# Routed expert kernel: the low halves of w1 prepared earlier, a softmax set eight steps later, one weight request moved ahead of another

## The chip, the cores and the metric

The kernel runs on one core of a Trainium2 chip. The metric is the device time of one execution in microseconds (us). Every run here is of the whole kernel, from its inputs in DRAM to its output in DRAM.

## The reference

The reference has two stages. The first is a causal convolution along the sequence whose seven weights differ at every position and head; they come from a softmax over the seven raw weights. The second is a mixture of 16 experts in 4 groups of 4: each token picks a group, then an expert of it, runs through that expert's two matrices and is scaled by the product of the two gate weights.

```python
w = np.exp(weight_gen - np.max(weight_gen, axis=-1, keepdims=True))
w = w / (np.sum(w, axis=-1, keepdims=True) + 1e-09)          # B=8, S=2880, 8 heads, K=7
out = np.einsum('bshk,bskhg->bshg', w, x_unf)                # x_unf: the 7 last rows of x, D=192
x = out.reshape(23040, 192)
g_idx = np.argmax(x @ w_group, axis=1)
...
e_idx = np.argmax(xg @ w_expert[g], axis=1)
...
h = np.maximum(xg[mask_e] @ w1[g, e], 0.0)                   # w1: 192 x 1024
ye = h @ w2[g, e]                                            # w2: 1024 x 192
out[tok_idx] = combined[:, None] * ye
```

## The kernel before

**Convolution.** The 23040 tokens lie as 128 partitions of 180. They are worked in 15 groups of 12 columns (two chunks of 6). For each group the SP queue loads the raw weights `wt` and the rows `xin` (`load_group`, lines 119 and 129; two buffers of each, so the load of group g+1 waits until group g-1 is done with its buffers). `softmax` (lines 260 to 280) turns `wt` into weights: maximum (L265), subtraction (L267), exponential on ScalarE (L268), sum (L273), reciprocal (L277), product (L279). `conv` multiplies by each of the seven taps on VectorE (L294). In the first three groups TensorE adds the products up (L335) and ScalarE copies the sums out (L338); from group 3 on VectorE adds them itself (L312).

**Routing.** `logits` transposes the convolved rows and scores them on TensorE (L392, L393, L375, L419), with copies on ScalarE between (L385, L399, L411, L422). `ranks` picks group and expert on VectorE (L346 to L360, then `oh` at L449), counts on TensorE (L459, L460) and gives each token a row in DRAM; GpSimd scatters the rows (L503). `table` (L528 to L586) then lists blocks of rows for a round.

**Experts.** 14 rounds give a list of blocks in a fixed order. Round 0 (after group 1) has ten singles (128 rows, block numbers 0 to 9), the rounds after it have doubles (256 rows, from block 10 on), the last one has ten triples, six doubles and two singles and a remainder. A block loads its rows `xb` (L779), its first matrix and its second (L803), and runs gemm1 (L907) and gemm2 (L945) in four or eight units. A single loads the first matrix straight into a tile `wa` (L790; three tiles in turn). A larger block loads it raw (`raw`, L792 and L799) and splits it into a rounded part, made by ScalarE (L816, L825), and a rest, made by VectorE (L840). One of the loads at L799 reads `w1lo` from DRAM.

**Low halves.** `w1lo` holds the rest of the last 64 rows of w1 and is made once by `halves`, in eight pairs of experts. For pair k: SP fetches it (`fetch`, L610); ScalarE makes the negative rounded copy (L602); SP stores the fetched rows to DRAM (L604); GpSimd adds the negative copy onto them with an accumulating DMA (L605). The tiles for this are borrowed from `wa`, `wc` and `raw`. `HALVES` holds the due time of each fetch on the planner's own clock; the low half of pair k-1 is made right after fetch k.

**Order.** The program order on TensorE, ScalarE, VectorE and SP is written out by a planner while the kernel is built. It keeps a clock for each engine with a fixed cost for each step. `front` yields the steps of the convolution; between two of them `beside` moves low halves, then the next group's softmax (the list `side`), then the routing. `blocks` writes out the expert units and fills with steps of `front` up to TensorE's clock plus a lead. Requests for loads stand in a list, and `pump` writes them out in order on the SP queue, which runs in program order, so a load that waits holds all that stand behind it. `state["slots"]` becomes true when the first double is taken up. `FIRST` is 2.

Of the kernel before, what the change touches and what calls it, by code (L numbers as in the profile page):

```python
# [22 lines left out]
AHEAD = (1.0, 1.0, 2.5)  # L23
HURRY = 12
SPACED = range(2, 15)
HALVES = (36.0, 42.0, 48.0, 54.0, 60.0, 66.0, 72.0, 78.0)
WHOLE = 12
SINGLE = tuple((k,) for k in range(7))
MIXED = ((0, 1), (2,), (3,), (4,), (5,), (6,))
# [12 lines left out]
def conv_moe_kernel(ctx: ExitStack, tc: tile.TileContext, x, wgen, w_group, w_expert, w1, w2, out):  # L42
# [27 lines left out]
    ENDS = [r[0] for r in ROUNDS]  # L70
# [6 lines left out]
    FIRST = ENDS[0]  # L77
# [151 lines left out]
    state = {"slots": False, "open": False, "unit": 0, "starve": False, "ph": 0, "hold": False}  # L229
# [360 lines left out]
    def halves():  # L590
# [9 lines left out]
        def lower_half(k):  # L600
            e, hi, raw = 2 * k, his[k % len(his)], raws[k]
            nc.scalar.activation(out=hi, in_=raw, func=AF.Copy, scale=-1.0)  # L602
            low = w1lo[e:e + 2].rearrange("e p f -> (e p) f")
            nc.sync.dma_start(out=low, in_=raw)  # L604
            nc.gpsimd.dma_start(out=low, in_=hi.bitcast(F32), accum_op=ALU.add)  # L605
            run("pool", 1.1, run("act", 1.0))

        def fetch(k):
            for h in range(2):
                nc.sync.dma_start(out=raws[k][h * HP:(h + 1) * HP, :], in_=w1v[2 * k + h, P:D, :])  # L610

        yield NEXT
        for k, raw in enumerate(raws):
            yield Until(HALVES[k])
            fetch(k)
            if k == 0:
                continue
            lower_half(k - 1)
        yield Until(HALVES[-1] + 6.0)
        lower_half(len(raws) - 1)  # L620
# [16 lines left out]
    def front():  # L637
        side = []
        set_up()
        load_group(1)  # L640
        next(slow[0][0])
        yield from softmax(0, 0, SC)
        rest = softmax(0, SC)

        def pace(g):
            return 99 if g <= FIRST else HURRY if g < MAIN + 3 else 8 if g in ENDS else 2

        def beside(g, n):
            rush = g >= FIRST and not grp[FIRST - 1].routed
            if not rush:  # L650
                for q in list(slow):
                    yield from move(slow, q, 2)
            for q in side[:1]:
                if not rush:
                    yield from move(side, q, 3)
            yield from routing(g)

        def routing(g):
            if ranking:
                yield from move(ranking, ranking[0], pace(g))  # L660
            if scoring and (not ranking or g < FIRST):
                yield from move(scoring, scoring[0], pace(g) if scoring[0][2].chunks == 2 or g >= FIRST - 1 else 3)

        def settle(g):
            while not grp[g].routed:
                qs = ranking or scoring
                q = qs[0]
                yield from move(qs, q, 99)
                if qs and qs[0] is q and q[1] is not None:
                    yield Until(q[1][1]) if q[1][0] == "time" else NEXT  # L670

        for g in range(ENDS[-1]):
            o = grp[g]
            o.routed = False
            scoring.append([logits(g, o), None, o])
            for n, c in enumerate(conv(g, o)):
                yield c
                if g == 0 and n < 6:
                    for c in islice(rest, None if n == 5 else 1):
                        yield c  # L680
                if n == (2 if state["slots"] else 0) and 1 <= g < ENDS[-1] - 1:
                    load_group(g + 1)
                if n >= (12 if state["slots"] else 4) and not o.ahead and g + 1 < ENDS[-1] and g != FIRST - 1:
                    o.ahead = True
                    side.append([softmax(g + 1), None])
                yield from beside(g, n)
                if g == FIRST - 1 and n in (7, 8):
                    if n == 7:
                        soft = softmax(FIRST)
                    yield next(soft)  # L690
            if g == FIRST - 1:
                for n, c in enumerate(soft):
                    yield c
                    yield from beside(g, n)
            yield from finish_all(side)
            if g:
                yield from settle(g - 1)
        yield from settle(ENDS[-1] - 1)
# [59 lines left out]
    def plain(n):  # L758
        return order[n][1] == 1
# [229 lines left out]
    def blocks(n0, n1, paced):  # L989
# [24 lines left out]
        def ask_w(n):  # L1014
            ask(n, 1)
            ask(n, 2)
# [66 lines left out]
        for i in range(len(units) + LAG):  # L1083
            if i < len(units):
                n, u = units[i]
                last = units_of(n) - 1
                gemm1(cur, u)
                queue.append((cur, u))
                nxt_at = i + last + 1 - u
                if nxt_at < len(units):  # L1090
                    if u == 0:
                        pump(units[nxt_at][0])
                        nxt = block(nxt_at)
                        prep_d(nxt)
                    if u == 1:
                        prep_x(nxt, 0)
                    if u == last // 2 + 1 and nxt.nt > 2:
                        prep_x(nxt, 2)
                if u == last and i + 1 < len(units):
                    cur = nxt  # L1100
            asks = []
            if i >= LAG:
                b, u = queue.pop(0)
                gemm2(b, u)
                if u == units_of(units[i - LAG][0]) - 1:
                    finish(b)
                    if i - LAG + 1 < len(units):
                        asks.append(units[i - LAG][0] + 3)
            if i < len(units):
                n, at = units[i]  # L1110
                end = at == last
                if end and n + 3 < n1 and (plain(n + 3) or plain(n + 2)):
                    ask_w(n + 3)
                    if not plain(n + 3):
                        ask_w(n + 4)
                did = 0
                for job in list(jobs):
                    m, part, h = job
                    if m > n + 2 or (part == 3 and (m > n + 1 or at < LAG)):
                        continue  # L1120
                    must = end and m == n + 1
                    if not must and (did >= 1 or (m, part) in want or not ready(m)):
                        continue
                    jobs.remove(job)
                    work_split(job)
                    did += 1
                state["unit"] += 1
            flush()
            if paced:
                fill(clk["pe"] + AHEAD[0 if cur.plain else 1 if cur.o.whole else 2])  # L1130
            for a in asks:
                ask_x(a)
            pump()
# [45 lines left out]
```

## Time and profile before

| | |
|---|---|
| median of 3 runs | 1201.04 us (1196.92, 1201.04, 1202.0) |
| profiled execution | 1193.24 us, span of the trace 1191.6 us |
| TensorE busy (matmul) | 1132.8 us, 95% of the span |
| VectorE busy | 959.7 us, 81% |
| ScalarE, GpSimd busy | 651.2 us (55%), 569.1 us (48%) |
| DMA | 275.08 MB, mean 231 GB/s |

The profiled execution is 7.80 us shorter than the median of the runs, and 3.68 us shorter than the fastest of them. Times of the trace count from the span's start.

### The profile page before, as it was taken

How to read it: one execution, taken by the hardware profiler on the slowest of the kernel's cores; microseconds unless marked ns; L12 is line 12 of the kernel's file. 1: busy time of each engine (PE TensorE's matmuls, PEld its weight loads, DVE VectorE, ACT ScalarE, POOL GpSimd, SP SyncE). 2: the span in 40 equal slices, each digit the busy share in tenths (PEclk: the TensorE clock that was granted, in tenths of full speed). 3: DMA queues.
4: the chain of work that ended last, by engine and by line, in shares of the span. 5: the costliest groups of instructions: out<-in, count | busy, mean ns of one | idle time of the engine just before them, and what ended most of it. 6: DMA issues, size and time to landing. Idle time of an engine off the chain costs nothing.

```text
span 1191.6 us, 24474 instructions
## 1 busy us (share of the span) xinstructions
PE 1132.8 (95%) x8357; PEld 1073.7 (90%) x8357; DVE 959.7 (81%) x1646; ACT 651.2 (55%) x1235; POOL 569.1 (48%) x608
## 2 busy tenths in 40 slices
PE   5787899999999999999999999999999989999998
PEld 3444788999999999999999999999899989999997
DVE  8899898999998999899999999898535756666661
ACT  1331345565565655655655655655556766666572
POOL 6154183756273747575656555374664112222211
PEclk9997999999999999999999999999999999999999
DMA  5698799887888877888687878558688675555562
GB/s 172 212 308 224 264 303 308 267 266 249 255 253 261 282 221 239 274 253 264 211 298 228 281 223 293 186 160 257 203 271 256 217 196 159 160 161 159 164 200 76
DMA packets 82758, 275.08 MB, mean 231 GB/s; under 512 B 15063, under 2 KB 31734, under 8 KB 80832
## 3 DMA queue, kind: packets, MB, share of 16 engines
q1 hardware_dynamic: 62296, 229.76, 61.9%
q0 software_dynamic: 20208, 43.39, 11.5%
q8 instruction: 67, 1.10, 0.4%
q14 instruction: 67, 0.55, 0.2%
q10 hardware_dynamic: 120, 0.28, 0.1%
HBM read 225.83 MB, written 48.42 MB: 230 GB/s over the span
## 4 chain that ended last, share of the span: by engine, by line
PE 58%; issue 20%; DVE 7%; DMA 6%; POOL 5%; SPq 2%; ACT 1%; POOLq 1%; DVEq 0%; ACTq 0%
PE py L945 26%; PE ph L907 24%; POOL out L962 4%; DVE pr L294 3%; PE pl L375 2%; DMA raw<-w1lo 1%; PE tpx L882 1%; DMA out<-y,xb 1%; PE tpx L881 1%; DMA wt<-in_weight_gen 1%; DMA w1lo<-raw 1%; DMA xb<-rows 1%; PE ph L335 1%; PE tp L392 1%; POOLq L557 1%
## 5 line engine op out<-in xcount | busy, mean ns | idle before, releaser
L907 PE MATMUL ph<-xh,wa 128*128 128x256 f32 (+1 forms) x1992 | 465.5, 307 | 0.0
L962 POOL DMA_INDIRECT out<-y,xb x189 | 204.9, 1084 | 438.7 <-DVE y L960 193.8
L945 PE MATMUL py<-wc,hh 128*128 128x192 f32 x2160 | 399.9, 326 | 2.1 <-ACT y L954 2.1
L907 PE MATMUL ph<-xl,wa 128*128 128x256 f32 (+1 forms) x1328 | 360.2, 290 | 0.3 <-DVE xl L840 0.3
L945 PEld LDWEIGHTS py<-wc,hh 128*128 128x128 f32 x2160 | 346.4, 190 | 2.4 <-ACT y L954 2.3
L907 PEld LDWEIGHTS ph<-xh,wa 128*128 128x128 f32 x1992 | 337.5, 190 | 3.3 <-issue 1.8
L913 ACT ACTIVATE hh<-ph 128x512 f32<-128x512 f32 (+2 forms) x296 | 165.5, 559 | 262.0 <-PE ph L907 261.8
L294 DVE TENSOR_TENSOR pr<-xin,wt 128x1152 f32<-128x1152 f32 x186 | 248.9, 1350 | 5.5 <-PE py L335 3.5
L907 PEld LDWEIGHTS ph<-xl,wa 128*128 128x128 f32 x1328 | 251.9, 190 | 0.6 <-DVE xl L840 0.6
L503 POOL DMA_INDIRECT rows<-xrow,ix x156 | 227.4, 1457 | 49.4 <-POOL ix L502 35.8
L312 DVE TENSOR_TENSOR xrow<-xrow,pr 128x1152 f32<-128x1152 f32 x144 | 194.6, 1351 | 0.7
L840 DVE SCALAR_TENSOR_TENSOR pr<-ph,hh 128x384 fp32r<-128x384 f32 (+1 forms) x128 | 77.5, 606 | 99.8 <-ACT hh L918 98.6
L840 DVE TENSOR_TENSOR wa<-raw,wa 128x1024 fp32r<-128x1024 f32 x83 | 101.4, 1222 | 31.1 <-ACT wa L816 30.9
L947 PE MATMUL py<-wc,hh 128*128 128x384 f32 x352 | 110.6, 362 | 0.0
L918 ACT ACTIVATE hh<-ph 128x384 fp32r<-128x384 f32 (+1 forms) x128 | 68.4, 534 | 69.8 <-PE ph L907 69.8
L502 POOL COPY ix<-posi 128x1 int32<-128x1 int32 x156 | 70.0, 458 | 63.7 <-DMA rows<-xrow,ix 36.2
L816 ACT CAST wa<-raw 128x1024 fp32r<-128x1024 f32 x83 | 87.2, 1050 | 3.1 <-DMA raw<-in_moe_w 3.1
L948 PE MATMUL py<-wc,pr 128*128 128x192 f32 x352 | 88.0, 250 | 0.0
L825 ACT CAST wa<-raw 128x1024 fp32r<-128x1024 f32 x83 | 86.7, 1045 | 0.6 <-DMA raw<-w1lo 0.6
L954 ACT ACTIVATE y<-py,xb 128x192 f32<-128x192 f32 x179 | 67.1, 422 | 21.4 <-PE py L945 19.7
L840 DVE TENSOR_TENSOR xl<-tpx,xh 128x512 fp32r<-128x512 f32 (+1 forms) x94 | 61.5, 655 | 17.0 <-ACT xh L887 16.2
L948 PEld LDWEIGHTS py<-wc,pr 128*128 128x128 f32 x352 | 67.1, 191 | 0.0
(178 smaller groups left out, 1341.8 us busy)
## 6 DMA issues: line engine op xcount, KB each, us to landing
wc<-in_moe_w SPq DMA_DIRECT2D x73, 768.0 KB, 5.8
raw<-in_moe_w SPq DMA_DIRECT2D x83, 512.0 KB, 5.4
xin<-in_x SPq DMA_DIRECT2D x14, 1728.0 KB, 10.0
raw<-in_moe_w SPq DMA_DIRECT2D x91, 256.0 KB, 5.2
raw<-w1lo SPq DMA_DIRECT2D x83, 256.0 KB, 5.4
raw<-in_moe_w SPq DMA_DIRECT2D x22, 768.0 KB, 6.8
xb<-rows SPq DMA_DIRECT2D x72, 194.0 KB, 3.8
wa<-in_moe_w SPq DMA_DIRECT2D x24, 384.0 KB, 5.0
```

Source lines behind the costliest of these rows:

```text
L294: nc.vector.tensor_tensor(out=dst, in0=o.xin[:, c0 + k:c0 + k + SC, :].rearrange("p s (h g) -> p s h g", g=HG), in1=w4[:, c0:c0 + SC, :, k ...
L312: nc.vector.tensor_tensor(out=acc, in0=acc, in1=prs[k - 2], op=ALU.add)
L503: written_once(nc.gpsimd.indirect_dma_start(out=rows[:, :], out_offset=bass.IndirectOffsetOnAxis(ap=ix, axis=0), in_=src, in_offset=None, ...
L816: nc.scalar.copy(out=o.wa[:, 0, :], in_=o.raw[0])
L825: nc.scalar.copy(out=o.wa[:, 2, :], in_=o.raw[1])
L840: f(*a, **k)
L907: nc.tensor.matmul(ph[:, v, :], lhsT=w[:, f0:f0 + P], rhs=rhs, start=i == 0, stop=i == len(terms) - 1)
L913: nc.scalar.activation(out=hh, in_=ph, func=AF.Relu)
L945: nc.tensor.matmul(b.acc[t], lhsT=hh[:, v, c], rhs=wc[0][:, f, :], start=f == 0 and not (b.wide and t == 1), stop=f == NFT - 1 and not (b. ...
L947: nc.tensor.matmul(b.py[t], lhsT=hh[:, v, c], rhs=wc[f // 4][:, f % 4].rearrange("p l d -> p (l d)"), start=f == 0, stop=False)
L948: nc.tensor.matmul(b.acc[t], lhsT=hl[:, v, c], rhs=wc[f // 4][:, f % 4, 0, :], start=False, stop=f == NFT - 1)
L962: ins = nc.gpsimd.indirect_dma_start(out=out[:, :], out_offset=bass.IndirectOffsetOnAxis(ap=b.x.bitcast(I32)[:, t, D + 1:D + 2], axis=0), ...
```

## The change

It has three parts. The due times of the eight low halves go from 36 to 78 down to 22 to 53. The softmax of the next group, which was entered behind 4 steps of the convolution as long as no double had been taken up, is entered behind 12 steps in groups 3 and later; this touches groups 3 and 4 (the softmax of groups 4 and 5). At the end of a single whose third follower is the last single before a double, the raw first matrix of that double is requested, and ahead of the single's own tile; the request for the next double keeps its place. With the order of this kernel that is block 6, which asks for block 10 and then for block 9; before, block 7 asked for 10 and 11, and now it asks for 11 alone.

```diff
-HALVES = (36.0, 42.0, 48.0, 54.0, 60.0, 66.0, 72.0, 78.0)
+HALVES = (22.0, 26.0, 30.0, 34.0, 38.0, 43.0, 48.0, 53.0)
...
-                if n >= (12 if state["slots"] else 4) and not o.ahead and g + 1 < ENDS[-1] and g != FIRST - 1:
+                if n >= (12 if state["slots"] or g > FIRST else 4) and not o.ahead and g + 1 < ENDS[-1] and g != FIRST - 1:
...
-                if end and n + 3 < n1 and (plain(n + 3) or plain(n + 2)):
+                if end and n + 4 < n1 and plain(n + 3) and not plain(n + 4):
+                    ask_w(n + 4)
                     ask_w(n + 3)
-                    if not plain(n + 3):
-                        ask_w(n + 4)
+                elif end and n + 3 < n1 and plain(n + 3):
+                    ask_w(n + 3)
+                elif end and n + 4 < n1 and plain(n + 2):
+                    ask_w(n + 4)
```

## Rows read from the trace of the kernel before

**Rows 1.** Stages: busy time of each engine, granted clock, DMA share, GB/s.

```profile
28.00:36.00 8.00, 6.12 (x36) 3.65 (x37) 7.97 (x7) 1.62 (x4) 0.00 (x0) 1.00 0.00 0
36.00:46.00 10.00, 8.88 (x59) 5.13 (x58) 7.99 (x9) 3.29 (x7) 0.00 (x0) 1.00 0.85 275
...
95.00:127.00 32.00, 24.57 (x122) 15.03 (x123) 26.80 (x30) 8.57 (x18) 12.48 (x12) 0.82 0.84 269
...
300.00:400.00 100.00, 100.00 (x807) 98.58 (x806) 91.19 (x168) 58.12 (x110) 50.42 (x52) 1.00 0.82 251
```

**Rows 2.** TensorE in order of time, around its two longest waits.

```profile
126.94 1.06 PE L907 MATMUL ph<-xd,wa 96*128 96x128 f32 x8
...
141.06 0.24 PE L459 MATMUL pl<-oh,tri 128*128 128x192 bf16 x1 [1.80 <-DVE oh L449]
...
192.58 0.92 PE L945 MATMUL py<-wc,hh 128*128 128x192 f32 x4 [2.13 <-ACT y L954]
```

**Rows 3.** What TensorE waited for, 127 to 205 us: total, times, longest.

```profile
PE py L945 <- ACT y L954: 2.1, 1, 2.1
PE pl L459 <- DVE oh L449: 1.8, 1, 1.8
PE pl L393 <- ACT rem L385: 0.7, 1, 0.7
```

**Rows 4.** What TensorE waited for, 320 us to the end.

```profile
PE tpx L881 <- DVE xl L840: 3.4, 1, 3.4
```

**Rows 5.** VectorE in order of time; idle before, and its releaser, in brackets.

```profile
52.05 0.85 DVE L265 TENSOR_REDUCE m<-wt 128x96 f32<-128x672 f32 x1
...
120.68 1.35 DVE L294 TENSOR_TENSOR pr<-xin,wt 128x1152 f32<-128x1152 f32 x1
125.44 0.85 DVE L265 TENSOR_REDUCE m<-wt 128x96 f32<-128x672 f32 x1 [3.40 <-DMA wt<-in_weight_gen]
...
147.74 0.15 DVE L586 TENSOR_SCALAR tab<-ri 128x1 int32<-128x1 f32 x1
...
174.51 0.85 DVE L265 TENSOR_REDUCE m<-wt 128x96 f32<-128x672 f32 x1 [1.74 <-DMA wt<-in_weight_gen]
...
191.70 1.22 DVE L840 TENSOR_TENSOR wa<-raw,wa 128x1024 fp32r<-128x1024 f32 x1 [2.48 <-ACT wa L816]
```

**Rows 6.** Chain of waits, 95 to 130 us: start, length, what.

```profile
99.87 11.61 DMA w1lo<-raw
...
112.05 5.41 DMA w1lo<-wa
...
120.35 5.06 DMA wt<-in_weight_gen
```

**Rows 7.** The SP queue in order of time.

```profile
7.99 1.21 SPq L610 DMA_DIRECT2D wa<-in_moe_w  x2
36.51 0.33 SPq L119 DMA_DIRECT2D wt<-in_weight_gen  x1
...
169.99 1.02 SPq L803 DMA_DIRECT2D wc<-in_moe_w  x1
178.80 0.87 SPq L790 DMA_DIRECT2D wa<-in_moe_w  x2
...
183.86 0.33 SPq L792 DMA_DIRECT2D raw<-in_moe_w  x1
```

**Rows 8.** ScalarE in order of time.

```profile
50.05 1.06 ACT L602 ACTIVATE wa<-wa 128x1024 fp32r<-128x1024 f32 x1 [1.41 <-DMA wa<-in_moe_w]
...
190.62 1.04 ACT L816 CAST wa<-raw 128x1024 fp32r<-128x1024 f32 x1 [3.14 <-DMA raw<-in_moe_w]
```

**Rows 9.** What VectorE waited for, 115 to 205 us.

```profile
DVE m L265 <- DMA wt<-in_weight_gen: 5.1, 2, 3.4
DVE wa L840 <- ACT wa L816: 3.2, 2, 2.5
```

**Rows 10.** DMA issues, 0 to 230 us: size each, median us to landing.

```profile
wa<-in_moe_w SPq DMA_DIRECT2D x6, 256.0 KB, 12.3
```

## The prediction

> **What bounds the kernel now.** I began with the busy time by stage, to learn which engine sets the end and from when. From 300 us on TensorE is busy for all of each 100 us, at full clock, with VectorE at 91 of 100 [rows 1]. Between 95 and 127 us TensorE is at 24.57 of 32 and its mean granted clock is 0.82, so the load passes to it in that stretch: from 126.94 us, where the second unit of the first single starts, the expert units follow one another [rows 2]. From there on an edit is worth only what it takes out of TensorE's idle time, or what it moves that start. So the second view was TensorE's waits. Behind 127 us and before 205 us two of them are long and single: 2.1 us for ScalarE's output copy and 1.8 us for VectorE's `oh`; the rest are round trips of the routing through ScalarE of 0.7 us and less [rows 3]. From 320 us to the end the longest wait is 3.4 us [rows 4]. Third, I followed these two waits back, on VectorE, ScalarE and SP.
>
> The wait of 1.8 us. The counting matmul L459 comes up in TensorE's order and `oh` is not there until 141.06 [rows 2]. VectorE makes it late because it stood for 3.40 us in front of the softmax of group 4, whose raw weights landed at 125.4 [rows 5]. The chain of waits says why those were late: the eighth low half is stored for 11.61 us, accumulated for 5.41 us, and its tile is the `wa` tile that the third single is to load; that load stands on SP ahead of group 4's weights, which go out at 120.35 only and take 5.06 us more [rows 6].
>
> The wait of 2.1 us. The raw matrix of block 10 is requested at 183.86, behind the tile of block 9, which stood on SP until its buffer came free at 178.80 [rows 7]. ScalarE reaches the rounding of that matrix, waits 3.14 us for it [rows 8], and an output copy of a single stands behind it; the matmul that needs the copied bank starts at 192.58 after 2.13 us of waiting [rows 2].
>
> **Part 1, low halves earlier.** It removes nothing and adds nothing: eight fetches, eight roundings, eight stores and eight accumulating DMAs stay. Five of the fetches come ahead of group 2's loads on SP, and all eight are due ahead of group 1's routing, so the eighth leaves the stretch from 99.87 to 117.46 [rows 6]. SP then waits for the scattered rows only before it goes on to group 4's weights. For TensorE this is worth between 0 and the 1.8 us of the first wait; part 2 takes the same wait, and it counts once.
>
> What hides the work in its new place: from 28 to 36 us the DMA share is 0 [rows 1], because the next loads can't go before group 0 has freed its buffers at 36.51 [rows 7]. One low half moves 0.52 MB (128 x 1024 numbers of 4 bytes) three times: fetch, store, accumulate. At the 275 GB/s of the stretch from 36 to 46 us [rows 1] that is 1.57 / 0.275 = 5.7 us each and 46 us for eight, an estimate; the idle 8 us take only one or two of them. The others run beside the loads of groups 1 and 2. There `wt` is first read at 52.05 [rows 5], 15.5 us after its issue, and `xin` a group later; so they are covered, unless landing takes three times the 5.06 us of [rows 6]. On ScalarE the roundings of pairs 4 to 7 stand about where those of pairs 0 to 3 stood, and one of those waited 1.41 us for its fetch [rows 8]. The bounds are a gain of 1.41 us and a loss of that for each of the late ones, 5.6 us; I take 0, since the fetches now go out earlier against the same places.
>
> The Trainium skill, page "DMA: Bandwidth & Descriptors", section "Issuing engines are not separate DMA queues", speaks against this part: transfers started by different engines run on the same 16 DMA engines and interleave, so GpSimd's accumulates would take time from SP's loads. The trace agrees as far as that the share reaches 0.85 with both under way. By that page alone, group 2's 2.1 MB (by its tiles) at half rate would take 15 us in place of 7.6, landing where the first read stands, which changes the sum by 0 to 2 us.
>
> **Part 2, softmax behind 12 steps.** The same instructions come eight steps later, 8 x 1.3 = 10 us of convolution, at 1.35 us for a product [rows 5] less what overlaps. Products and sums take their place. Group 4's weights landed 3.40 us too late and group 5's 1.74 us too late [rows 5], 5.1 us together [rows 9]; 10 us more cover both. TensorE gets 1.8 us of the first, the whole of its wait at L459, since `oh` comes 3.4 us or more earlier. It gets nothing of the second: the next counting matmul has no wait of its own among the waits of that stretch [rows 3]. Bounds: 0 and 5.1 us; I take 1.8, because TensorE's own queue is full from 126.94 on. Late next is TensorE itself. The cost where the cover is gone: group 5's softmax (five pieces of up to 0.85 us [rows 5], some 4.2 us) now stands near block 10's splitting L840; that piece sat idle 2.48 us before [rows 5], and VectorE arrives there 5 us earlier, so I cost it at 0.
>
> **Part 3, raw matrix of block 10 first.** Three DMAs move on SP from 183.86 to right behind 169.99 [rows 7], past the tile load that waits until 178.80 for its buffer. Behind them stand that load, the rows and the second matrix of block 9; they wait for three issues, about 1.6 us, in a stretch in which SP stands still for 8 us anyway. The raw buffers are free (the low halves are long done), and the table of round 1, from which SP reads the expert's number, is written at 147.74 [rows 5]. Landing took 190.62 - 183.86 = 6.8 us [rows 7, 8]; from 171 us it is there by 178, ten us ahead of use. The 3.14 us of ScalarE and the 2.1 us of TensorE go. Bounds: 0 (if the output copy is late for another reason) and 3.14 us; I take 2.1.
>
> **Sum.** 0 + 1.8 + 2.1 = 3.9 us, all of it ahead of a TensorE that is full: 1193.24 - 3.9 = 1189.3 us for an execution like the profiled one. That one lies 7.80 us below the median of the runs, so on the median the forecast is 1201.04 - 3.9 = 1197.1 us, -0.3%. A difference under about 0.5% (6 us) is what a measurement of this kernel can't tell from no change.
>
> **Rivals.**
>
> *VectorE's idle time comes through whole.* 5.1 + 3.2 = 8.3 us of waits go from VectorE [rows 9]. If the rounds to come hang on the convolution, not on TensorE, all of it counts: 1192.7 us. For it: VectorE is at 91% even at 300 us, and of the chain from 95 to 130 us that one load is 5.06 us [rows 6]. Against it: TensorE waits for nothing long up to 320 us, and beyond it once, 3.4 us [rows 3, 4].
>
> *Another wait steps in.* TensorE's order is fixed at building; with the softmax moved, a chunk of groups 3 and 4 is complete earlier and its routing is written between other units, with round trips of 0.7 us each [rows 3]. Two or three such trips more, or a copy that is late for block 10's rows, take most of the gain: 0 to 1.5 us are left, 1200.3 us.
>
> *Slower: the low halves hold SP.* The store of a low half waits at the head of SP for its fetch, and group 2's loads stand behind the fourth store. A fetch took 12.3 us to land in the median [rows 10]. The first goes out at 7.99, and two are in flight at a time: they land at about 20 us and the next two at 33, ahead of 36.51 [rows 7]. If landing takes over 13 us the fourth store outlasts the buffers' release; at 20 us group 2's `wt` goes out at 49 and lands between 54 (5.06 us later) and 61 (12.3 us), against its read at 52.05 [rows 5]: up to 9 us lost on VectorE ahead of the first single, less the 3.9 gained, 1206 us. For it: eight low halves are 46 us of DMA time. Against it: the DMA stands still there before.
>
> **Chances and range.** Forecast 0.52, VectorE's whole 0.20, another wait 0.15, slower 0.13. The likeliest gives 1197.1, with a range of its own of 1193 to 1201 (its 3.9 us from the fastest run shown, and none of it from the median). Over all cases: down to VectorE's 8.3 us taken from the fastest run, 1188.6, and up to 1204, which leaves out the last of the slow case. Faster by over 0.5%: nearly all of the second case and a fifth of the first, 0.29. Slower: three quarters of the last, 0.10. Within: 0.61.
>
> **What would show it.** Right: no wait of L265 for `wt` over 0.5 us in groups 4 and 5; all stores of low halves ahead of 70 us; L459 and L945 gone from TensorE's list; `raw` of block 10 issued near 170 us; the second unit of the first single still at about 127 us; the trace shorter by about 4 us. Wrong: that unit moves by over 2 us either way, which would say that the front does depend on the low halves; a new wait of 1 us or more on TensorE between 127 and 320 us; or a gain that grows beyond 320 us, which would make VectorE the bound.

## The result: slower by 0.9%

| | median | lowest to highest | runs |
|---|---|---|---|
| kernel before | 1199.29 us | 1196.06 to 1204.48 | 7 |
| changed kernel | 1209.16 us | 1207.15 to 1211.9 | 7 |

The ratio is 1.0088 with a 95% interval of 1.0065 to 1.0110: some 10 us slower, where 3.9 us less were forecast and 1204 us was the range's end. The profiled execution took 1209.13 us (span 1207.4 us), against 1193.24 (1191.6) before. The traces differ by 15.8 us, more than the medians by 9.9, because the execution profiled before was one of the quickest, 6.05 us under the median of its runs. Ratios, here and below, are formed from the runs in the faster of the chip's two states alone and need not equal the quotient of the medians shown.

### The profile page after: what moved, and what is told of

It reads as the page before. It is cut to its first block, busy times and chain, and to the rows that moved or that the text cites. A ratio compares the mean times of both kernels' runs of the same rounds, so it can differ in the third digit from the quotient of the medians.

```text
span 1207.4 us, 24465 instructions
## 1 busy us (share of the span) xinstructions
PE 1135.8 (94%) x8357; PEld 1077.7 (89%) x8357; DVE 959.8 (79%) x1646; ACT 651.3 (54%) x1235; POOL 581.1 (48%) x608
## 4 chain that ended last, share of the span: by engine, by line
PE 62%; issue 20%; DMA 5%; DVE 5%; POOL 4%; ACT 2%; SPq 1%; POOLq 0%; DVEq 0%; ACTq 0%
PE py L945 27%; PE ph L907 26%; POOL out L962 4%; DVE pr L294 2%; PE pl L375 2%; DMA raw<-in_moe_w 1%; PE tpx L882 1%; DMA raw<-w1lo 1%; PE tpx L881 1%; DMA out<-y,xb 1%; DMA xb<-rows 1%; PE tp L392 1%; PE pl L392 1%; DMA xin<-in_x 1%; ACT xT L399 1%
## 5 line engine op out<-in xcount | busy, mean ns | idle before, releaser
L907 PE MATMUL ph<-xh,wa 128*128 128x256 f32 (+1 forms) x1992 | 467.1, 308 | 0.0
L962 POOL DMA_INDIRECT out<-y,xb x189 | 230.7, 1221 | 424.9 <-DVE y L960 192.1
L945 PE MATMUL py<-wc,hh 128*128 128x192 f32 x2160 | 402.0, 327 | 0.0
L907 PE MATMUL ph<-xl,wa 128*128 128x256 f32 (+1 forms) x1328 | 361.2, 291 | 0.0
L945 PEld LDWEIGHTS py<-wc,hh 128*128 128x128 f32 x2160 | 348.8, 191 | 0.0
L907 PEld LDWEIGHTS ph<-xh,wa 128*128 128x128 f32 x1992 | 338.7, 191 | 3.3 <-issue 1.8
L907 PEld LDWEIGHTS ph<-xl,wa 128*128 128x128 f32 x1328 | 252.9, 190 | 0.1
L503 POOL DMA_INDIRECT rows<-xrow,ix x156 | 219.0, 1404 | 48.8 <-POOL ix L502 35.6
L502 POOL COPY ix<-posi 128x1 int32<-128x1 int32 x156 | 63.9, 420 | 80.5 <-DMA rows<-xrow,ix 45.6
L954 ACT ACTIVATE y<-py,xb 128x192 f32<-128x192 f32 x179 | 67.3, 423 | 21.9 <-PE py L945 20.2
```

The costliest lines, as they stand in the source:

```text
L503: written_once(nc.gpsimd.indirect_dma_start(out=rows[:, :], out_offset=bass.IndirectOffsetOnAxis(ap=ix, axis=0), in_=src, in_offset=None, ...
L907: nc.tensor.matmul(ph[:, v, :], lhsT=w[:, f0:f0 + P], rhs=rhs, start=i == 0, stop=i == len(terms) - 1)
L945: nc.tensor.matmul(b.acc[t], lhsT=hh[:, v, c], rhs=wc[0][:, f, :], start=f == 0 and not (b.wide and t == 1), stop=f == NFT - 1 and not (b. ...
L962: ins = nc.gpsimd.indirect_dma_start(out=out[:, :], out_offset=bass.IndirectOffsetOnAxis(ap=b.x.bitcast(I32)[:, t, D + 1:D + 2], axis=0), ...
```

## The profile after

The stages. Columns: stretch, its length, busy time of the engines, granted clock of TensorE, DMA share, GB/s.

```profile
36.00:46.00 10.00, 8.88 (x62) 5.04 (x54) 7.99 (x9) 4.49 (x9) 0.85 (x1) 1.00 1.05 249
95.00:127.00 32.00, 23.59 (x76) 12.87 (x74) 29.35 (x49) 7.62 (x16) 14.10 (x12) 0.90 0.68 222
...
200.00:204.00 4.00, 3.89 (x18) 3.88 (x18) 2.92 (x4) 3.18 (x7) 2.17 (x3) 0.57 1.03 323
...
208.00:212.00 4.00, 2.39 (x20) 2.13 (x18) 2.40 (x5) 4.00 (x8) 1.66 (x3) 1.00 1.05 321
212.00:216.00 4.00, 3.24 (x18) 3.00 (x19) 4.00 (x5) 1.81 (x5) 3.26 (x4) 0.72 1.05 289
784.00:788.00 4.00, 3.93 (x17) 3.62 (x18) 2.44 (x3) 3.39 (x7) 1.31 (x3) 0.60 1.01 370
```

Three of the stretches of 4 us shown run below full clock (0.57, 0.72, 0.60), with 17 or 18 matmuls each. Each stands behind a gap, as TensorE's timeline of the changed kernel shows (in brackets the idle time and what ended it; L872 transposes the rows of a single, L881 those of a larger block, L393 part of a group's convolved rows for the routing):

```profile
130.07 1.06 PE L907 MATMUL ph<-xd,wa 96*128 96x128 f32 x8
...
142.22 0.25 PE L459 MATMUL pl<-oh,tri 128*128 128x192 bf16 x1
...
191.50 0.42 PE L872 MATMUL tp<-ident,xb 128*96 128x128 f32 x2 [1.65 <-DMA xb<-rows]
199.68 0.33 PE L881 MATMUL tpx<-ident,xb 128*128 128x128 f32 x1 [1.58 <-DMA xb<-rows]
212.52 0.33 PE L393 MATMUL tp<-ident,rem 128*128 128x128 f32 x1 [2.13 <-ACT rem L385]
238.21 0.33 PE L393 MATMUL pl<-ident,rem 128*128 128x128 f32 x1 [1.64 <-ACT rem L385]
...
783.96 0.47 PE L881 MATMUL tpx<-ident,xb 128*128 128x128 f32 x1 [5.70 <-DMA xb<-rows]
```

The two waits that the forecast went after are gone: L459 stands without idle time, and no wait of L945 for `y` is left in the stretch of [rows 3]. In their place are two waits for a block's rows (block 9 at 191.50, block 10 at 199.68), two for `rem`, a copy that ScalarE makes for the routing, and at 784 us one of 5.70 us for rows.

Where the time goes is plain when the same matmul is looked up in both traces. Each trace holds 3704 records of gemm1 (L907); the table gives the start of a few of them before, and by how much each is later in the changed kernel, in a second profiled execution of the changed kernel, and in four variants that the experiments below explain, all on chips on which the kernel before takes 1200 us.

| start before, us | changed | changed, 2nd | group 4 alone | own row buffer | group 3 alone | group 3 + part 3 |
|---|---|---|---|---|---|---|
| 126.9 | +3.1 | +0.2 | -2.2 | +0.1 | -0.5 | +0.4 |
| 146.3 | +1.2 | -1.8 | -1.0 | 0.0 | -2.4 | -1.5 |
| 182.6 | +1.2 | -1.8 | +0.3 | 0.0 | -2.4 | -1.5 |
| 194.9 | +0.6 | -2.6 | -0.6 | -1.4 | +3.4 | -2.3 |
| 248.8 | +9.6 | +8.6 | +5.7 | +7.3 | +4.5 | -1.8 |
| 760.9 | +8.7 | +7.7 | +4.8 | +2.6 | +4.5 | -1.7 |
| 774.1 | +17.0 | +16.7 | +13.4 | +3.2 | +4.5 | -1.7 |
| 1172.6 | +15.8 | +17.1 | +15.9 | +1.1 | +5.1 | -2.3 |

The changed kernel loses in two places: 9.0 us between 195 and 249 us (second execution 11.2), and 8.3 us at 784 (9.0). From 249 to 761 us the distance changes by 0.9 us only: TensorE is full. These differences are taken against the one trace of the kernel before on such a chip, a quick execution; where an execution at the median of its runs loses its 6 us more isn't known.

**The place at 784 us.** It is a row load. GpSimd's timeline before, and then of the changed kernel (L503 scatters the convolved rows, L962 a block's output):

```profile
760.98 0.97 POOL L962 DMA_INDIRECT out<-y,xb  x1 [7.42 <-ACT y L954]
762.26 0.97 POOL L962 DMA_INDIRECT out<-y,xb  x1 [0.30 <-ACT wa L825]
764.24 0.98 POOL L503 DMA_INDIRECT rows<-xrow,ix  x1 [0.15 <-POOL ix L502]
```

```profile
768.18 0.98 POOL L503 DMA_INDIRECT rows<-xrow,ix  x1 [0.15 <-POOL ix L502]
...
774.33 1.81 POOL L503 DMA_INDIRECT rows<-xrow,ix  x1 [0.28 <-POOL ix L502]
...
776.75 1.92 POOL L962 DMA_INDIRECT out<-y,xb  x1 [0.15 <-issue]
778.98 0.97 POOL L503 DMA_INDIRECT rows<-xrow,ix  x1 [0.30 <-issue]
780.25 0.98 POOL L962 DMA_INDIRECT out<-y,xb  x1 [0.30 <-issue]
```

Before, the output scatters go first. In the changed kernel five scatters of rows, which wait for the routing, are written ahead of them. GpSimd works through its list in order here: ScalarE has copied this block's output out (L954) by 769.73, and it leaves at 776.75, right behind the last of the five. The buffer `xb` of that block, which a triple three places later is to load into (three buffers in turn), is free only when it has left. SP's load stands waiting for that scatter; first before, then changed (waits of SP from 700 to 800 us: total, times, longest; then the issue):

```profile
SPq L779 <- DMA out<-y,xb: 11.0, 3, 9.2
...
763.50 0.34 SPq L779 DMA_DIRECT2D xb<-rows  x1
```

```profile
SPq L779 <- DMA out<-y,xb: 24.4, 2, 18.2
...
780.22 0.34 SPq L779 DMA_DIRECT2D xb<-rows  x1
```

Before, TensorE reaches that triple at 769.08, 5.6 us after the issue. In the changed kernel it is there at 783.96 - 5.70 = 778.26, ahead of the issue.

**The places at 191 to 240 us.** The raw matrix of block 10 now goes out early (L792 on SP, with its two companions at L799), but the rows of block 9 are loaded late, at 188.96 (before at 182.18), behind output scatters that left GpSimd at 180.72 to 184.63, and behind them on SP those of block 10, at 193.24 (before at 189.55):

```profile
172.33 0.63 SPq L792 DMA_DIRECT2D raw<-in_moe_w  x1
...
179.96 0.87 SPq L790 DMA_DIRECT2D wa<-in_moe_w  x2
188.96 0.35 SPq L779 DMA_DIRECT2D xb<-rows  x1
...
193.24 0.34 SPq L779 DMA_DIRECT2D xb<-rows  x1
```

The routing copy `rem` of 211.93 stands on ScalarE behind the exponential of the moved softmax (L268, 0.76 of the 2.13 us that TensorE waits), the rounding of a raw matrix and other work of the blocks:

```profile
208.12 1.05 ACT L816 CAST wa<-raw 128x1024 fp32r<-128x1024 f32 x1
209.07 0.76 ACT L268 ACTIVATE wt<-wt 128x672 f32<-128x672 f32 x1
...
211.00 1.06 ACT L825 CAST wa<-raw 128x1024 fp32r<-128x1024 f32 x1
211.93 0.54 ACT L385 COPY rem<-xrow 128x384 f32<-128x384 f32 x1
```

**Part 1 in the front.** The sixth pair's fetch goes out at 38.05, behind group 2's loads, and its rounding waits on ScalarE for 6.71 us with `exg`, a step of the routing, behind it:

```profile
55.80 1.06 ACT L602 ACTIVATE wc<-raw 128x1024 fp32r<-128x1024 f32 x1 [6.71 <-DMA raw<-in_moe_w]
56.77 0.23 ACT L352 ACTIVATE exg<-ls 128x48 f32<-128x48 f32 x1
```

VectorE waits for that (list of its waits, 30 to 100 us; total, times, longest):

```profile
DVE smg L446 <- ACT exg L352: 5.3, 1, 5.3
```

The first single starts at 119.41 instead of 115.01. In the second execution the same rounding waited 3.38 us and the first single started at 116.44.

## The experiments

The theory after the first look was that part 1 carries the loss, through the rounding that holds ScalarE and the late front. The rival was that part 2 carries it, through the order that the planner now writes: row scatters ahead of output scatters. All kernels compute the whole result. The runs up to the first group-4 one were made on three chips on which the kernel before takes 1229 to 1235 us, the last six on two with 1200 us; ratios are always against the kernel before on the same chip.

**The parts one by one.** Each kernel takes the lines of its part from the change's diff.

```diff
-HALVES = (36.0, 42.0, 48.0, 54.0, 60.0, 66.0, 72.0, 78.0)
+HALVES = (22.0, 26.0, 30.0, 34.0, 38.0, 43.0, 48.0, 53.0)
```

```diff
-                if n >= (12 if state["slots"] else 4) and not o.ahead and g + 1 < ENDS[-1] and g != FIRST - 1:
+                if n >= (12 if state["slots"] or g > FIRST else 4) and not o.ahead and g + 1 < ENDS[-1] and g != FIRST - 1:
```

```diff
-                if end and n + 3 < n1 and (plain(n + 3) or plain(n + 2)):
+                if end and n + 4 < n1 and plain(n + 3) and not plain(n + 4):
+                    ask_w(n + 4)
...
```

What was expected of part 1, part 2, part 3, and parts 2 and 3 together:

> The low halves' due times of the change alone, the rest as before. Theory (ScalarE's order): the rounding of the sixth pair stands on ScalarE ahead of the exponential that routing group 0 needs, waits 5 to 7 us for its fetch behind group 2's loads, VectorE waits about 5 us at L446, and the second unit of the first single comes 3 to 4 us later than before (126.94); the wait at L459 gets shorter, so the whole is 1 to 3 us slower, ratio 1.001 to 1.003. Rival (the loss lies in the planner's new order, part 2): VectorE catches up behind the front, ratio 0.998 to 1.001.

> The softmax behind 12 steps alone. Theory: the front is as before, the wait at L459 goes (-1.8 us), and group 5's softmax falls among ScalarE's work for the first doubles, where the routing's copy L385 comes late (+3 to 4 us): ratio 1.000 to 1.003. Rival (part 2 carries the loss, since it changes the written order of all that follows): +6 us or more, ratio 1.005 to 1.009.

> The raw matrix of block 10 asked ahead of block 9's tile alone. Theory: the 2.1 us wait at L945 goes, but 1 MB of raw weights now lands beside the scatters; the output scatter that frees block 9's row buffer lands late, SP stands at that row load for 5 us or more, and the rows of blocks 9 and 10 come late by 1.5 us each: ratio 1.000 to 1.003. Rival (the row loads were late for the front's delay only): the 2.1 us stay gained, ratio 0.997 to 0.999.

> Parts 2 and 3 without the low halves. Theory: the changed kernel less the front's 3 us: ratio 1.004 to 1.007. Rival (low halves carry it all, the two parts gain what was forecast): 0.996 to 0.998.

| | median, us (before 1229.46) | ratio, 95% interval |
|---|---|---|
| part 1 | 1228.12 | 0.9984, 0.9959 to 1.0008 |
| part 2 | 1236.81 | 1.0058, 1.0029 to 1.0087 |
| part 3 | 1225.57 | 0.9970, 0.9942 to 0.9998 |
| parts 2 and 3 | 1233.60 | 1.0050, 1.0020 to 1.0081 |

The theory fell: part 1 alone costs nothing that shows, although VectorE's wait for `exg` is there (3.6 us). Part 2 alone is slower. Its list of TensorE's waits has the late rows, and so has that of parts 2 and 3; those of parts 1 and 3 alone have none of over 1.6 us:

```profile
PE tpx L881 <- DMA xb<-rows: 6.7, 3, 5.7
```

**A row buffer of its own for the late triple.** If the load waits because it shares the buffer, another buffer takes the wait away with the order left as it is. To make room for it, the group's rows get four buffers instead of five; a control has this alone. The kernel before, unchanged, ran beside them for a trace of that chip, and a fourth kernel puts part 1's due times later, to take away the wait of ScalarE.

```diff
-        o.xrow = [cv.tile([P, SC, W], F32, name="xrow", bufs=5) for _ in range(WIDTHS[g] // SC)]
+        o.xrow = [cv.tile([P, SC, W], F32, name="xrow", bufs=4) for _ in range(WIDTHS[g] // SC)]
...
+    xown = const.tile([P, 3, W], F32, name="xown")
-            o.xb = xbs[n % 3][:, h:h + nb, :]
+            o.xb = xown if nb == 3 and r < NR - 1 else xbs[n % 3][:, h:h + nb, :]
```

```diff
-HALVES = (22.0, 26.0, 30.0, 34.0, 38.0, 43.0, 48.0, 53.0)
+HALVES = (22.0, 26.0, 30.0, 34.0, 38.0, 50.0, 56.0, 62.0)
```

Expected of the kernel before again, of the changed kernel with four buffers, with the own buffer too, and with the later due times:

> The kernel before, on the chip of this call, to have its trace beside those of the others. Both theories: no wait of TensorE for `xb` over 1 us behind 600 us, and the second unit of the first single near 127 us.

> The changed kernel with four buffers for the convolved rows in place of five, which frees the room that the next run needs; the control of that run. All theories: as the changed kernel, slower than before by 0.5 to 0.9%, with a wait of 5 to 6 us for `xb` near 780 us.

> As the control, but the one triple ahead of the last round has row buffers of its own, so that its load doesn't wait for the output scatter of the block three before it. Theory (part 2 moves a group's row scatters on GpSimd ahead of that output scatter, and the triple's rows come late): the wait of 5 to 6 us near 780 us goes and 6 to 8 us with it against the control, ratio 1.000 to 1.003. Rival (the rows are late for the DMA load or for the SP queue): the wait stays at 3 us or more, and the ratio within 0.002 of the control's.

> The changed kernel with the last three low halves due at 50, 56 and 62 in place of 43, 48 and 53; the first five stay early. Theory (the sixth pair's rounding stood at ScalarE's head while its fetch was under way, and the exponential behind it held VectorE): the 5 us wait at L446 goes, the first singles start 3 to 4 us earlier than in the changed kernel, ratio 0.002 to 0.004 below it. Rival (the fetches themselves are the load that delays the front): the front stays late, ratio as the changed kernel.

Against 1234.32 us before: the control 1241.04 (ratio 1.0104, 1.0037 to 1.0171), with the own buffer 1227.57 (0.9964, 0.9926 to 1.0002), with later due times 1242.32 (1.0090, 1.0048 to 1.0131). The control has four runs only. The kernel before again took 1231.22. The buffer turns the loss into a gain; it took off 13.5 us where 6 to 8 were expected. By the starts of the same matmuls 7.8 us of it go at the place of the 784 us, and 6.1 in the 80 us behind it, where the control waits 3.7 and 2.5 us for nothing that the profile shows. The later due times took VectorE's wait for `exg` away and gained nothing, but that trace has another stall in the front (4.60 us that the profile puts down to nothing), so it settles nothing about `exg`; part 1 alone, which has that wait and costs nothing that shows, speaks against it.

**Is the buffer good for any order, and is it enough for part 2?** The buffer's edit on the kernel before, on parts 1 and 3, on part 2 alone; and part 2 for group 4 alone, with the shared buffers.

```diff
-                if n >= (12 if state["slots"] else 4) and not o.ahead and g + 1 < ENDS[-1] and g != FIRST - 1:
+                if n >= (12 if state["slots"] or g == 4 else 4) and not o.ahead and g + 1 < ENDS[-1] and g != FIRST - 1:
```

Expected of the kernel before, of parts 1 and 3, of part 2 (each with the own buffer), and of group 4 alone:

> The kernel before, with four buffers for the group's rows instead of five and with a row buffer of its own for the one triple ahead of the last round (the edit of the changed kernel's run with its own row buffer, on the kernel before). Theory, the shared row buffer costs time only in the order that part 2 writes: the kernel before has no wait of TensorE on the triple's rows (none over 0.5 us), so nothing is to be had here: ratio to before 0.997 to 1.003. Rival, the buffer of its own is worth as much in any order: ratio 0.987 to 0.992 (13 us less, as between the two runs of the changed kernel). Expected: the first.

> Parts 1 and 3 without part 2, with the own row buffer of the triple and four row buffers of a group. Theory: with part 2 away neither the late rows nor the late routing is there; parts 1 and 3 alone measured 0.998 and 0.997, together 0.995, or 0.992 to 0.998. Rival, the parts hinder each other in the front (the late raw weights of part 1 meet the earlier raw asks of part 3): ratio 1.000 to 1.004.

> Part 2 alone, with the own row buffer of the triple and four row buffers of a group. Theory, the loss of part 2 is the triple's late rows (5.7 us, 7.6 with the half clock after them): ratio to before 0.997 to 1.001 instead of 1.006, the wait on the triple's rows at 2 us or less. Rival, part 2 loses as much by its late routing copies and its gaps in the front: ratio 1.004 or more, with the wait on the triple's rows gone too.

> Part 2 for one group alone: the softmax of the group after group 4 stands behind 12 steps, that after group 3 behind 4 as before. If the last moved softmax alone is what puts the row scatters ahead of the output scatters on GpSimd, the 5.7 us wait on the triple's rows is there and the ratio is 1.003 to 1.007. If it takes the earlier one too, the wait is absent or below 1 us and the ratio is 0.996 to 1.002. I hold the first slightly likelier (0.55), for the routing that came late in the changed kernel was that of group 4.

| | median, us (before 1235.30) | ratio, 95% interval |
|---|---|---|
| before, own buffer | 1236.70 | 1.0002, 0.9968 to 1.0035 |
| parts 1 and 3, own buffer | 1231.11 | 0.9965, 0.9933 to 0.9998 |
| part 2, own buffer | 1229.28 | 0.9957, 0.9930 to 0.9984 |
| part 2 for group 4 alone | 1243.44 | 1.0044, 1.0007 to 1.0081 |

The buffer is worth nothing to the kernel before and 1.0% to part 2. And group 4's softmax alone brings the wait. Waits of TensorE for rows, first part 2 with the own buffer (its lines are numbered one higher), then group 4 alone:

```profile
PE tpx L882 <- DMA xb<-rows: 2.4, 2, 1.9
```

```profile
PE tpx L881 <- DMA xb<-rows: 7.2, 3, 5.8
```

**Group 3's softmax, and the changed kernel once more**, on a chip on which the kernel before takes 1200 us.

```diff
-                if n >= (12 if state["slots"] else 4) and not o.ahead and g + 1 < ENDS[-1] and g != FIRST - 1:
+                if n >= (12 if state["slots"] or g == 3 else 4) and not o.ahead and g + 1 < ENDS[-1] and g != FIRST - 1:
```

Expected of this, of this with part 3, and of the changed kernel:

> Part 2 for group 3 alone: the softmax of the group after group 3 stands behind 12 steps, that after group 4 behind 4 as before. If the late rows and the late routing copies hang on the last moved softmax alone (group 4's run showed 7.2 us of waits on the triple's rows), both are absent here: wait of TensorE on the triple's rows under 1 us, on the routing copies at 213 to 238 us under 1 us each, and the ratio is 0.994 to 0.999, the gain of part 2 (the L459 wait of 1.8 us on the first chip, 4 to 5 us with the half clock on this one) without its loss. If either softmax alone shifts the order, the row wait is 5 us or more and the ratio is 1.003 to 1.007.

> Group 3's softmax behind 12 steps and part 3, without part 1 and without the moved softmax of group 4: the two gains that were measured, without the row wait. Sum of the two: 0.992 to 0.997. If the two edits get in each other's way (row loads of blocks 9 and 10 late behind the raw weights): 0.998 to 1.002.

> The changed kernel itself, beside the others of this call. If the loss is in the order of its instructions, it stays: ratio 1.004 to 1.012, the 5.7 us wait on the triple's rows there, and the waits on group 4's routing copies (2 us each) at 212 and 238 us. If the 9 us that the first trace of it had lost by 250 us belonged to that one execution or chip, its first 250 us are at most 3 us behind the kernel before on this chip; if they belong to the kernel, 6 us or more behind.

| | median, us (before 1199.92) | ratio, 95% interval |
|---|---|---|
| group 3's softmax | 1198.21 | 0.9988, 0.9968 to 1.0007 |
| group 3's softmax and part 3 | 1194.09 | 0.9950, 0.9927 to 0.9973 |
| changed kernel | 1208.92 | 1.0067, 1.0040 to 1.0093 |

Waits of TensorE with group 3's softmax alone: the late rows are gone, and the one for a single's output copy, which stands on ScalarE behind the rounding of block 10's raw matrix, is larger than before (2.13 us in [rows 2]).

```profile
PE py L945 <- ACT y L954: 5.9, 1, 5.9
...
PE tpx L881 <- DMA xb<-rows: 0.8, 2, 0.4
```

TensorE comes 2.4 us earlier to a matrix that is not requested earlier. With part 3 it is, the wait is gone, and the kernel stays 1.5 to 2.3 us ahead through all the later rows of the table. On GpSimd the order is that of before again:

```profile
760.52 0.97 POOL L962 DMA_INDIRECT out<-y,xb  x1 [0.30 <-ACT wa L825]
762.50 0.98 POOL L503 DMA_INDIRECT rows<-xrow,ix  x1 [0.15 <-POOL ix L502]
```

The changed kernel's second trace has the loss at 195 to 249 us and the one at 784 us in their old places:

```profile
782.88 0.48 PE L881 MATMUL tpx<-ident,xb 128*128 128x128 f32 x1 [5.64 <-DMA xb<-rows]
```

**The two losses apart**, on the other such chip. The own buffer; the changed kernel with group 3's softmax moved and group 4's not; group 4's alone.

The one edit not shown yet is that of the second, against the changed kernel:

```diff
-                if n >= (12 if state["slots"] or g > FIRST else 4) and not o.ahead and g + 1 < ENDS[-1] and g != FIRST - 1:
+                if n >= (12 if state["slots"] or g == 3 else 4) and not o.ahead and g + 1 < ENDS[-1] and g != FIRST - 1:
```

> The changed kernel with the own row buffer of the triple once more. On the chip of the earlier run it gave 0.9964; there the kernel before lost some 10 us by 270 us that it does not lose in its first trace. If this run is on the first chip: the late rows at 784 us are gone (7.6 to 8.4 us of the trace), the 7.6 us lost at 200 to 250 us are not: ratio 1.000 to 1.003. If it is on the other chip: 0.994 to 0.999 again. The rival, that the row buffer is the whole of the loss, asks for 0.998 or less on either.

> The changed kernel without its moved softmax of group 4 (parts 1 and 3, and part 2 for group 3 alone). If group 4's moved softmax is the whole of the loss, both at 200 to 250 us and at 784: 0.994 to 0.998, beside 0.995 for the same without part 1, no row wait over 1 us. If part 1 hinders by its late front (first single 3 to 4 us later in the changed kernel): 0.999 to 1.002.

> Part 2 for group 4 alone once more, beside the two others. Ratio 1.003 to 1.009 on either chip, with the row wait of 5.6 to 5.8 us and the 2 us wait on the routing copies near 213 us.

| | median, us (before 1200.23) | ratio, 95% interval |
|---|---|---|
| changed kernel, own buffer | 1196.06 | 0.9962, 0.9934 to 0.9990 |
| changed kernel, group 4 as before | 1198.95 | 0.9992, 0.9965 to 1.0020 |
| group 4's softmax alone | 1209.82 | 1.0085, 1.0051 to 1.0120 |

With group 4 as before 0.994 to 0.998 was expected if its softmax were the whole of the loss, and 0.999 to 1.002 if part 1 delayed the first single. The ratio of 0.9992 lies at the near end of the second, yet the first single is not late in that trace (115.18). Its matmuls start 0.1 us behind those of the kernel before from 249 to 855 us; then one wait of 1.7 us for rows (expected: none over 1 us) comes at 912 us.

Group 4's moved softmax alone is as slow as the whole change. Its GpSimd order and the matmul that pays for it:

```profile
770.42 1.80 POOL L503 DMA_INDIRECT rows<-xrow,ix  x1 [0.28 <-POOL ix L502]
772.84 1.92 POOL L962 DMA_INDIRECT out<-y,xb  x1 [0.15 <-issue]
```

```profile
780.13 0.48 PE L881 MATMUL tpx<-ident,xb 128*128 128x128 f32 x1 [5.78 <-DMA xb<-rows]
```

With the own buffer the ratio fell further than I expected for such a chip (1.000 to 1.003): it is 1.05% or 12.6 us below that of the changed kernel. The table of starts says from where. At 774 us it loses 0.6 us instead of 9.0. The 8.7 us between 195 and 249 us are still lost. But from 249 to 761 us it comes 4.7 us closer (+7.3 to +2.6), a stretch in which the changed kernel comes 0.9 us closer. Gemm1 is quicker there: 300 to 700 us, groups of instructions, mean ns of one behind the busy time, the changed kernel's second trace and then the own buffer:

```profile
L907 PE MATMUL ph<-xh,wa 128*128 128x256 f32 x858 | 194.4, 303 | 0.0
L907 PE MATMUL ph<-xl,wa 128*128 128x256 f32 x572 | 149.1, 282 | 0.0
```

```profile
L908 PE MATMUL ph<-xh,wa 128*128 128x256 f32 x864 | 193.4, 300 | 0.0
L908 PE MATMUL ph<-xl,wa 128*128 128x256 f32 x575 | 147.6, 279 | 0.0
```

3 ns for 1439 matmuls are 4.3 us. Why they are quicker stays open. Part 2 with the buffer has 300 and 279 ns too, the kernel before with the same buffer 303 and 283, both on a chip of 1235 us, so it isn't the buffer alone.

All 20 traces agree on the place at 784 us. In the eight with group 4's moved softmax and the shared buffers the matmuls behind it start 8.3 to 9.3 us later against the kernel before than those ahead of it, in the three with that softmax and the own buffer 0.6 us later, and in the others they move by 0.1 us or less.

## Why the prediction was wrong

**The step that failed** is the cost of part 2. The text moved "the same instructions eight steps later", looked for their cover on VectorE, took "0 and 5.1 us" as the bounds of a gain, and costed the rest at 0. No bound stood on the other side. What moved was not only the softmax: the planner wrote the whole later list anew. Two of the signs that the prediction had named came: the first single's second unit moved by 3.1 us (0.2 in the second execution), and waits of over 1 us stand between 127 and 320 us. The runs put the loss of part 2 at 0.58% alone, of group 4's half at 0.44 and 0.85%, and take it away with group 4 put back (0.9992; without part 1 0.9950). In the traces it has two terms. Late rows at 784 us: 5.7 us of waiting and about 3 us of lower clock behind it, 8.3 to 9.0 us. Gaps at 195 to 249 us: 9.0 and 11.2 us in the changed kernel, 6.3 with group 4 alone, 0.5 and 1.2 without group 4 (the second with part 1). The first term is shown by the own buffer, on both kinds of chip. Of the second it is shown that its two waits of L393 for ScalarE (2.1 to 2.8 and 1.6 us) stand in all eleven traces with group 4's moved softmax and in none of the other nine. The waits for the rows of blocks 9 and 10 are another matter: in the traces of group 3's softmax with part 3, group 4 as before, block 9's is there with 1.25 and 1.38 us, and with group 4's softmax alone neither is. That the copies `rem` are late because the exponential stands ahead of them on ScalarE is read from timelines and not tried; it is 0.76 us long.

What the second term costs in time is less certain than the first. On the chip of the buffer runs the kernel before, traced there once with 1231 us, is itself 10.8 us late at the row of 248.8 in the table, with a wait of 3.0 us at L459 among others; the control, traced on the same chip, is 9.1 us late there. At 760.9 the two stand at 31.5 and 32.5 us, and at 774.1 at 31.5 and 40.9: the distance comes from the late rows. So 9.0 and 11.2 us are what the second term costs against a quick execution of the kernel before, on the chips of 1200 us.

**The rival "another wait steps in"** named the mechanism, routing written between other units and copies late for block 10's rows, but let it take only the gain, 0 to 1.5 us left. It looked for it between 127 and 320 us. The dearest single wait came 460 us later, where TensorE has been full for hundreds of us and no instruction had been edited.

**Part 2's gain** was right: L459's wait is gone, and from 126.9 to 146.3 us the changed kernel gains 1.9 us (second trace 2.0), against 1.8. Group 3's softmax brings it alone (1.9). In the two traces of the last chip that hold it together with part 1, only 0.1 us shows in this stretch: the wait is gone there too, but TensorE's granted clock is 0.50 from 126 to 130 us (1.00 in the changed kernel's two). Group 5's weights, late by 1.74 us, gave TensorE nothing, as argued; the half of part 2 that serves them is the half that costs.

**Part 3's gain** was right in sign: 0.997 alone, and 0.38 points between group 3's softmax without and with it (4.1 us between their medians), against 2.1. In the changed kernel's own trace it shows as 0.6 to 0.8 us between 182.6 and 194.9, since the wait for block 9's rows, of 1.65 and 1.44 us, falls into the same stretch. The two gains hang together, which the sum did not see: without part 3, group 3's softmax turns into a wait of 5.9 us at L945.

**Part 1** was taken as 0 within a gain of 1.41 and a loss of 5.6 us. The row that the loss was worked out from had 1.41 us; the changed kernel waits 6.71 and 3.38 us in one rounding. Of that the first single's second unit shows 3.1 and 0.2 us. In the two traces of the last chip with part 1, the first single starts at 115.2 and 115.3, as before. In time, part 1 alone is 0.9984; the pair with and without it (0.9992 and 0.9950) leans to a loss of some 0.4%, from different sets of runs on two chips. It stays open between these two. The Trainium skill, page "DMA: Bandwidth & Descriptors", section "Issuing engines are not separate DMA queues", spoke against this part. The share of 0.85 in [rows 1], which the prediction took for agreement, is SP's work alone: GpSimd's first accumulating DMA stands at 52.02 in the trace before. The trace of the changed kernel agrees: from 36 to 46 us the share is 1.05, GpSimd's DMA queue moves 1.44 MB and SP's 1.03 MB (before 2.73 MB, alone), and the sixth pair's fetch takes 55.80 - 38.05 = 17.75 us to the rounding that waits for it, against a median of 12.3 [rows 10]. It didn't delay group 2's first read, as the forecast by that page had it, but the rounding. What made this a wait of VectorE is the order on ScalarE: `exg` stands at 56.77, right behind the rounding at 55.80. The Trainium skill, page "Perfetto Trace Analysis", section "Tensor Engine Instruction (MATMUL, LD_WEIGHTS)", says that ScalarE, VectorE and GpSimd work strictly in order; the trace agrees.

**The rivals "VectorE's idle comes through whole" and "the low halves hold SP"** did not come. Group 4's and 5's weights no longer hold L265, and the time is longer; and SP's first load for group 2 went out at 36.97 (36.51 before [rows 7]).

**The best version** of those that ran is group 3's softmax behind 12 steps with part 3, part 1 and group 4 left as they were: 0.9950 of the kernel before, 5.8 us, and 14.8 us less than the changed kernel beside it. Part 2 and the changed kernel with the own buffer, 0.9957 and 0.9962, lie within its interval.

## What to carry to other kernels

Where a planner writes the order, an edit early in the list is priced only when its reorderings are followed to the end: compare the written order on every queue, GpSimd's among them, before and after. Look for a buffer whose release stands behind work of another kind on an in-order queue; a spare buffer there, with a control for the room it takes, tells whether that shared buffer is the cost. Try the two halves of a condition (here group 3 and group 4) one by one: one held the gain, the other the loss at the late rows.

## What the runs showed of the hardware that I had not expected

Three of the five long gaps of the changed kernel were followed by a stretch near the lower clock level (1.2 of 2.4 GHz): 0.57 behind the 1.58 us at 199.68, 0.72 behind the 2.13 us at 212.52, 0.60 behind the 5.70 us at 783.96, where 8.3 us came out of a wait of 5.7. Behind the 1.65 us at 191.50 and the 1.64 us at 238.21 the clock stayed at 1.00, and so it did in the trace before behind the 1.80 and 2.13 us of [rows 2]. So gaps of nearly the same length were followed by either level; the forecast priced each gap by its length.

In the experiments the kernel before took 1200 us on two chips and 1229 to 1235 on three others, 2.5 to 3% apart. The sign of each edit that ran on both kinds was the same (changed kernel with own buffer 0.9964 and 0.9962; group 4's softmax 1.0044 and 1.0085).
